# The second half's feed-forward products as pairs of 64-row products in the two halves of the array, each pair on two banks that are then crossed

## The chip, the cores and the metric

The kernel runs on one core of a Trainium2 chip. The metric is the device time of one execution in microseconds. Before the change, three runs gave a median of 1269.06 us (1267.8 to 1270.67).

## The reference: what is computed

A linear attention feeds a gated feed-forward layer. Eight batches of 576 tokens make 4608 tokens of 512 features (8 heads of 64); the hidden width is 1536.

```python
q_p, k_p = (phi(q), phi(k))                 # 64 -> 128, exp(+) and exp(-)
kv = np.einsum('bhsf,bhsd->bhfd', k_p, v)
num = np.einsum('bhsf,bhfd->bhsd', q_p, kv)
den = np.einsum('bhsf,bhf->bhs', q_p, z)[..., None] + 1e-06
x = (num / den)                              # as 4608 x 512
gate = 1.0 / (1.0 + np.exp(-(x @ w_gate)))
val = x @ w_val
out = (gate * val @ w_out).astype(np.float32)
```

## The kernel before

All large products are kept in float32r. Each operand is split in two, a high part and the rest (names ending in `h` and `l`), and each product is the sum of three: high by high, high by low, low by high.

The hidden width is cut into 12 blocks of 128, numbered j = 0 to 11. In the first half of the kernel, attention and blocks 0 to 3 run together; the feed-forward result of these four blocks is parked in DRAM (`yscr`). The second half, `rest_chunks` (L297 to L352), does blocks 4 to 11 for all tokens. It goes over 9 chunks C of 512 tokens, and in each over 8 blocks j: 72 steps. A step does, on TensorE:

- `mm_in` (L159) twice. The gate values g and the values v, each 128 hidden features by 512 tokens, each in a PSUM bank of its own, each the sum of 12 products: 4 slices of 128 input features, times the three of the split. The weight block is the stationary operand, the tokens x the moving one with 512 columns.
- `out_step` (L308) for the step before (`late`): for each of 4 groups of 128 tokens t, three products (`mm_out`, L169) of the gated values `hh`, `hl` (stationary) with the output weights (moving, 512 columns), added into bank `acc{t}`. The four banks `acc0` to `acc3` gather the 8 blocks of a chunk.

That makes 24 + 12 = 36 products of 512 columns a step, 2592 in all. After the v products of a step, `gated` (L177) turns g and v into `hh` and `hl`: Tanh and Exp of g on ScalarE (L182, L183), three operations on VectorE (L185 absolute value, L186 with v, L187), a cast to `hh` on ScalarE and the remainder `hl` on VectorE (`split`, L62 to L64). This chain runs while TensorE does the next products; its result is used only after the g and v products of the next step.

At the end of a chunk, four VectorE operations (L322) join the accumulators with the parked result, which SyncE fetched (L320), and the sums go to DRAM (L325). Also once a chunk, SyncE loads the tokens of a later chunk (L301), ScalarE casts them to `xh` and VectorE makes `xl` (`split`, 2048 columns each). The x tiles have two buffers, so this load starts when the chunk two before it has used its tokens for the last time.

The weights of blocks 4 to 11 come as float64 words. `load_weights` (L99) loads a tile of 512 KB (three buffers `wraw`), and `from_f64` (L76) rebuilds it with six VectorE operations (L81, L83, L88, L91, L94, L95) and one of ScalarE (L82); its high part goes through a DMA (L86) into `wh`. There are 24 such tiles, and those of the later blocks are rebuilt while the first chunk (C = 0) is running.

In the second half the order on TensorE is as written. The order on VectorE, ScalarE, SyncE and GpSimd is set by the scheduler at build time, from its own estimate of how long everything takes; each engine then runs its list in order.

Of the kernel before, what the change touches and what calls it, by code (L numbers as in the profile page):

```python
# [9 lines left out]
F32 = mybir.dt.float32  # L10
# [11 lines left out]
P = 128  # L22
# [23 lines left out]
def attention_moe(  # L46
# [19 lines left out]
    def behind(stack, marks):  # L66
        for m in marks:
            stack.enter_context(tc.issue_after(m.ins))
# [100 lines left out]
    def mm_out(acc, t, hs, j, first, last):  # L169
        (hh, hl, _), (wh, wl) = hs, weights[j]  # L170
        ts, ws = slice(t * P, t * P + P), slice(2 * DM, 3 * DM)
        for i, (a, w) in enumerate(((hh, wh), (hh, wl), (hl, wh))):
            nc.tensor.matmul(  # L173
                acc, a[:, ts], w[:, ws], start=first and i == 0, stop=last and i == 2
            )

    def gated(g, vl, w, mp, hb, name):  # L177
        u = mp.tile([P, w], F32, tag="u", name="u" + name)
        t = mp.tile([P, w], F32, tag="t", name="t" + name)
        hh = mp.tile([P, w], F32R, tag="hh", name="hh" + name, bufs=hb)  # L180
        hl = mp.tile([P, w], F32R, tag="hl", name="hl" + name, bufs=hb)
        act.activation(t, g, AF.Tanh, scale=0.5)  # L182
        act.activation(u, g, AF.Exp)  # L183
        tu = t.bitcast(U32)
        vec.tensor_scalar(tu, tu, 0x7FFFFFFF, None, op0=ALU.bitwise_and)  # L185
        vec.scalar_tensor_tensor(t, t, 1.0, vl, op0=ALU.add, op1=ALU.mult)  # L186
        vec.scalar_tensor_tensor(u, u, 1.0, t, op0=ALU.min, op1=ALU.mult)  # L187
        return hh, hl, split(hh, hl, u)
# [108 lines left out]
    def rest_chunks(js, xp, mp, ps_gv, ps_acc, load):  # L297
# [7 lines left out]
            split(xh, xl, raw)  # L305
            return xh, xl

        def out_step(C, i, hs):  # L308
            if i == 0:
# [4 lines left out]
            for t in range(CW // P):  # L314
                acc = accs[C][t]
                mm_out(acc, t, hs, js[i], i == 0, i == len(js) - 1)
                if i == len(js) - 1:
                    r = C * CW + t * P
                    y1 = mp.tile([P, DM], F32, tag="y1", name=f"yp_{C}_{t}", bufs=4)
                    nc.sync.dma_start(y1, yscr[r // CH][r % CH // P])  # L320
                    y = mp.tile([P, DM], F32, tag="y", name=f"y2_{C}_{t}", bufs=4)
                    vec.scalar_tensor_tensor(  # L322
                        y, acc, 0.5, y1, op0=ALU.mult, op1=ALU.add
                    )
                    nc.sync.dma_start(out[r : r + P, :], y)  # L325

        accs, late = {}, None
        for i, j in enumerate(js):
            if i == 1:
                with ExitStack() as stack:  # L330
                    behind(stack, marks)
                    xs = load_x(0)
            for m in range(3):
                marks = load(j, m)
        for C in range(NT // CW):
            nxt = None
            for i, j in enumerate(js):
                n = f"2_{C}_{j}"
                g = ps_gv.tile([P, CW], F32, tag="g", name="g" + n)
                vl = ps_gv.tile([P, CW], F32, tag="v", name="v" + n)  # L340
                mm_in(g, xs, j, 0, CW)
                mm_in(vl, xs, j, 1, CW)
                hs = gated(g, vl, CW, mp, 2, n)
                if late:
                    out_step(*late)
                late = (C, i, hs)
                if i == max(0, len(js) - 3) and (C + 1) * CW < NT:
                    with ExitStack() as stack:
                        behind(stack, () if C else marks)
                        nxt = load_x(C + 1)  # L350
            xs = nxt
        out_step(*late)  # L352


    ctx.enter_context(tc.manual_schedule(engines={mybir.EngineType.PE}))
    with ExitStack() as actx:
# [384 lines left out]
        def load(i):  # L741
            if i < N:
                load_k(i)
                load_q(i)
# [145 lines left out]
```

## Time and profile before

| | us |
|---|---|
| median of 3 runs | 1269.06 |
| the profiled execution, own time | 1269.45 |
| its span, first to last instruction | 1267.7 |
| TensorE matmul busy in the span | 1221.1 |
| VectorE busy | 788.4 |
| ScalarE busy | 522.6 |
| GpSimd busy | 0.7 |

1.75 us of the profiled execution lie outside its span. The second half begins at about 671 us and lasts to the end. PE is TensorE's matmul, PEld its weight loading, DVE VectorE, ACT ScalarE, POOL GpSimd, SP SyncE. Matmuls are pipelined: their recorded durations overlap, and the distance from start to start is the pace. A row of the timeline has the start, the time covered, the engine, the line, the operation, output and inputs, sizes, the count, and in brackets the idle time ahead of it and what ended it.

### The profile page before, as it was taken

The page shows a single profiled execution, that of the slowest core. Times are in us where ns is not written, and L with a number is a line of the kernel's source. Part 1 is how long each engine was busy: PE and PEld are TensorE (multiplying, and loading weights), DVE is VectorE, ACT ScalarE, POOL GpSimd, SP SyncE. Part 2 cuts the span into 40 slices and gives each one's busy share as a digit, 9 for nine tenths or more (in the row PEclk, how much of TensorE's full clock was granted, in tenths as well). Part 3 has the DMA queues.
Part 4 walks back from the last instruction along what each step waited for, and adds up shares of the span by engine and source line. Part 5 has one row for each costly group of instructions (what it writes and reads, how often), then busy time and mean ns, then how long its engine had stood idle before and what let it go on. Part 6 is the DMA issues. An engine that isn't in the chain of part 4 may idle for free.

```text
span 1267.7 us, 22794 instructions
## 1 busy us (share of the span) xinstructions
PE 1221.1 (96%) x9328; PEld 967.8 (76%) x9328; DVE 788.4 (62%) x1597; ACT 522.6 (41%) x1077; POOL 0.7 (0%) x6
## 2 busy tenths in 40 slices
PE   7778899999999999999989999999999999999998
PEld 4455577777778777777877888888888888888887
DVE  6998778887877878883997843424343434343333
ACT  4655555566656556564443322222222212222221
POOL 0000000000000000000000000000000000000000
PEclk9988899999999999999999999999999999999999
DMA  5567344343424334332756430203020202011010
GB/s 178 166 217 247 112 123 132 104 122 106 140 94 132 95 105 140 108 97 88 261 191 206 140 100 1 100 1 101 1 100 1 100 1 80 21 59 42 10 58 33
DMA packets 79123, 130.33 MB, mean 103 GB/s; under 512 B 17068, under 2 KB 36652, under 8 KB 79020
## 3 DMA queue, kind: packets, MB, share of 16 engines
q1 hardware_dynamic: 79020, 128.89, 31.5%
q8 instruction: 73, 1.20, 0.4%
q14 instruction: 30, 0.25, 0.1%
HBM read 90.86 MB, written 28.44 MB: 94 GB/s over the span
## 4 chain that ended last, share of the span: by engine, by line
PE 82%; DVE 12%; DMA 2%; ACT 2%; issue 1%; SPq 0%; DVEq 0%
PE acc L173 22%; PE g L166 16%; PE v L166 16%; PE gv L166 12%; PE kvz L537 5%; PE nm L589 4%; PE pq L420 2%; PE pk L430 2%; PE dp L602 2%; PE kvz L551 1%; PE pk L491 1%; DMA wraw<-w_moe 1%; DVE dk L454 1%; DVE mb L522 1%; DVE mx L441 1%
## 5 line engine op out<-in xcount | busy, mean ns | idle before, releaser
L173 PE MATMUL acc<-wh,hh 128*128 128x512 f32 x432 | 172.3, 399 | 3.2 <-ACT y L265 2.4
L166 PE MATMUL gv<-xh,wh 128*128 128x256 f32 x576 | 171.7, 298 | 0.0
L173 PE MATMUL acc<-wl,hh 128*128 128x512 f32 x432 | 169.2, 392 | 0.0
L166 PE MATMUL gv<-xl,wh 128*128 128x256 f32 x576 | 165.1, 287 | 4.0 <-DVE xl L213 4.0
L173 PE MATMUL acc<-wh,hl 128*128 128x512 f32 x432 | 168.7, 390 | 0.0
L166 PE MATMUL gv<-xh,wl 128*128 128x256 f32 x576 | 165.0, 287 | 0.0
L185 DVE TENSOR_SCALAR t<-t 128x512 uint32<-128x512 uint32 x72 | 30.7, 426 | 171.4 <-ACT t L182 171.1
L63 ACT CAST hh<-u 128x512 fp32r<-128x512 f32 x72 | 44.6, 619 | 219.8 <-DVE u L187 219.8
L166 PEld LDWEIGHTS gv<-xh,wh 128*128 128x128 f32 x576 | 112.0, 194 | 15.1 <-issue 13.1
L182 ACT ACTIVATE t<-g 128x512 f32<-128x512 f32 x72 | 43.0, 597 | 185.6 <-PE g L166 185.5
L166 PEld LDWEIGHTS gv<-xl,wh 128*128 128x128 f32 x576 | 112.2, 195 | 4.9 <-DVE xl L213 4.6
L166 PE MATMUL g<-xh,wh 128*128 128x512 f32 x288 | 113.0, 392 | 0.0
L166 PE MATMUL v<-xh,wh 128*128 128x512 f32 x288 | 112.6, 391 | 0.0
L166 PE MATMUL g<-xh,wl 128*128 128x512 f32 x288 | 112.5, 391 | 0.0
L166 PE MATMUL g<-xl,wh 128*128 128x512 f32 x288 | 112.5, 391 | 0.0
L166 PE MATMUL v<-xl,wh 128*128 128x512 f32 x288 | 112.3, 390 | 0.0
L166 PEld LDWEIGHTS gv<-xh,wl 128*128 128x128 f32 x576 | 112.2, 195 | 0.0
L166 PE MATMUL v<-xh,wl 128*128 128x512 f32 x288 | 112.1, 389 | 0.0
L186 DVE SCALAR_TENSOR_TENSOR t<-t,v 128x512 f32<-128x512 f32 x72 | 49.4, 686 | 97.9 <-PE v L166 97.9
L173 PEld LDWEIGHTS acc<-wh,hh 128*128 128x128 f32 x432 | 81.1, 188 | 26.6 <-issue 5.8
L173 PEld LDWEIGHTS acc<-wh,hl 128*128 128x128 f32 x432 | 81.1, 188 | 18.7 <-DVE hl L238 0.2
L173 PEld LDWEIGHTS acc<-wl,hh 128*128 128x128 f32 x432 | 81.3, 188 | 16.0
(99 smaller groups left out, 2136.8 us busy)
## 6 DMA issues: line engine op xcount, KB each, us to landing
wraw<-w_moe SPq DMA_DIRECT2D x36, 512.0 KB, 5.4
xl<-xs SPq DMA_DIRECT2D x34, 512.0 KB, 3.9
k<-k SPq DMA_DIRECT2D x32, 320.0 KB, 3.7
v<-v SPq DMA_DIRECT2D x32, 320.0 KB, 3.0
q<-q SPq DMA_DIRECT2D x32, 288.0 KB, 4.2
wh<-wtop SPq DMA_DIRECT2D x36, 256.0 KB, 2.3
ys<-y SPq DMA_DIRECT2D x36, 256.0 KB, 2.1
yp<-ys SPq DMA_DIRECT2D x36, 256.0 KB
```

The source lines that it names most:

```text
L63: a = act.copy(h, x)
L166: nc.tensor.matmul(o, a[:, ws], x[:, cs], start=i == 0, stop=i == 11)
L173: nc.tensor.matmul(acc, a[:, ts], w[:, ws], start=first and i == 0, stop=last and i == 2)
L182: act.activation(t, g, AF.Tanh, scale=0.5)
L185: vec.tensor_scalar(tu, tu, 0x7FFFFFFF, None, op0=ALU.bitwise_and)
L186: vec.scalar_tensor_tensor(t, t, 1.0, vl, op0=ALU.add, op1=ALU.mult)
L420: nc.tensor.matmul(pps[hd], wk[head(hd), :], x[head(hd), cs], start=True, stop=True)
L430: nc.tensor.matmul(pps[hd][:, t, :], kx[head(hd), t * P : t * P + P], wk[head(hd), :], start=True, stop=True,)
L441: vec.tensor_reduce(mx[:, :ns], pp[:, :ns, :], axis=AX.X, op=ALU.max, apply_absolute_value=True,)
L537: nc.tensor.matmul(kvz[o : o + Q, : 2 * F], vx[:, 2 * t + hd, o % D : o % D + Q], (e0, e1)[hd][:, t, :] if t < 4 else e2[:, 0, :], start=t ...
L589: nc.tensor.matmul(nms[hf][o : o + Q, :], w[:, sg, o : o + Q], es[sg][:, o // D, cs], start=sg == 0, stop=sg == 1, tile_position=(0, o),)
L602: nc.tensor.matmul(dp[o : o + Q, :], w[:, 2, z : z + Q], es[sg][:, hd, hf * HS : hf * HS + HS], start=sg == 0, stop=sg == 1, tile_position ...
```

## The change

Every product of 128 contracted rows in the second half becomes two of 64 rows: one in the upper half of the array (rows 0 to 63), one in the lower (rows 64 to 127). The new `halves_mm` issues them in pairs, an upper and a lower one in turn, and the two of a pair fill different banks. In one pass g takes its upper rows while v takes its lower rows; in a later pass the banks are crossed, v above and g below. The out products do the same with `acc0`, `acc1` against `acc2`, `acc3`. A step is now: 12 pairs for g above and v below, 6 pairs of the first half of `out_half` for the step before, 12 pairs for v above and g below, 6 pairs of its second half. `gated` comes after all four, so g and v end together, and its result is used after the 12 pairs of the next step's first pass. Only the very first step has no step before it and keeps its whole products.

Where a bank changes from one half of the array to the other, the new code puts a memset of one element on GpSimd (`marks`) that waits for the last product of the old half, and the first product of the new half waits for the memset. This makes 10 such memsets in nearly every step.

```diff
+    ROWS = slice(0, P // 2), slice(P // 2, P)
...
+    def halves_mm(top, bottom):
+
+        for pair in zip(top, bottom):
+            for r, (o, (a, x), start, stop) in enumerate(pair):
+                rs = ROWS[r]
+                mm = nc.tensor.matmul(o, a[rs, :], x[rs, :], start=start, stop=stop).ins
+                before = None if start else fills.get(id(o))
+                if before and before[1] != r:
+                    mark = marks.tile([1, 1], F32, tag="mark", name="mark")
+                    turn = pool.memset(mark, 0.0).ins
+                    for later, sooner in ((turn, before[0]), (mm, turn)):
+                        tc.add_manual_dep(
...
+                fills[id(o)] = mm, r, o
...
+        def out_half(C, i, hs, n):
...
+            parts = [
+                [
+                    x
+                    for t in ts
+                    for x in group(accs[C][t], terms_out(t, hs, js[i]), first, last)
+                ]
+                for ts in ((0, 1), (2, 3))
+            ]
+            halves_mm(*(parts[::-1] if n else parts))
...
-                mm_in(g, xs, j, 0, CW)
-                mm_in(vl, xs, j, 1, CW)
-                hs = gated(g, vl, CW, mp, 2, n)
                 if late:
-                    out_step(*late)
-                late = (C, i, hs)
+                    tg, tv = (terms_in(xs, j, m, CW) for m in range(2))
+                    halves_mm(group(g, tg, start=True), group(vl, tv, start=True))
+                    out_half(*late, 0)
+                    halves_mm(group(vl, tv, stop=True), group(g, tg, stop=True))
+                    out_half(*late, 1)
+                else:
+                    mm_in(g, xs, j, 0, CW)
+                    mm_in(vl, xs, j, 1, CW)
+                late = (C, i, gated(g, vl, CW, mp, 2, n))
...
-        out_step(*late)
+        for n in range(2):
+            out_half(*late, n)
```

TensorE, chunk 4, block 7, before: the last g product, the first and last lines of the v products, and what follows. (In the names `g2_4_7` is the g bank of chunk 4, block 7; `acc2_4_0` the accumulator of its first 128 tokens; the last number is only a count.)

```order
L166 MATMUL v2_4_7_10845<-xh2_4_10569,wh7_8842 128x512
L166 MATMUL v2_4_7_10845<-xl2_4_10570,wh7_8842 128x512
L166 MATMUL v2_4_7_10845<-xh2_4_10569,wl7_8843 128x512
L173 MATMUL acc2_4_0_10779<-wh6_8807,hh2_4_6_10823 128x512
L173 MATMUL acc2_4_0_10779<-wl6_8808,hh2_4_6_10823 128x512
L173 MATMUL acc2_4_0_10779<-wh6_8807,hl2_4_6_10824 128x512
L173 MATMUL acc2_4_1_10780<-wh6_8807,hh2_4_6_10823 128x512
```

TensorE at the same place with the change: the end of the first half of `out_half`, and then the first pairs of the crossed pass.

```order
L200 MATMUL acc2_4_1_12532<-wl6_8811,hh2_4_6_12702 128x512
L200 MATMUL acc2_4_3_12534<-wl6_8811,hh2_4_6_12702 128x512
L200 MATMUL acc2_4_1_12532<-wh6_8810,hl2_4_6_12703 128x512
L200 MATMUL acc2_4_3_12534<-wh6_8810,hl2_4_6_12703 128x512
L200 MATMUL v2_4_7_12712<-xh2_4_12164,wh7_8845 128x512
L200 MATMUL g2_4_7_12711<-xh2_4_12164,wh7_8845 128x512
L200 MATMUL v2_4_7_12712<-xl2_4_12165,wh7_8845 128x512
L200 MATMUL g2_4_7_12711<-xl2_4_12165,wh7_8845 128x512
```

Upper and lower products alternate, and each has a bank of its own. The v products now end only after the out products' first half, and next to the g products.

VectorE where chunk 0 passes into chunk 1, before. `xl2_2` is the token tile of chunk 2, `t2_1_4`, `u2_1_4`, `hl2_1_4` the gate chain of the first step of chunk 1, and `y2_0_0` to `y2_0_3` the four joins of chunk 0.

```order
L64 TENSOR_TENSOR xl2_2_9726<-xl2_2_9726,xh2_2_9725 128x2048
L185 TENSOR_SCALAR t2_1_4_9434<-t2_1_4_9434 128x512
L322 SCALAR_TENSOR_TENSOR y2_0_0_9449<-acc2_0_0_9091,yp_0_0_9447 128x512
L186 SCALAR_TENSOR_TENSOR t2_1_4_9434<-t2_1_4_9434,v2_1_4_9408 128x512
L322 SCALAR_TENSOR_TENSOR y2_0_1_9457<-acc2_0_1_9092,yp_0_1_9455 128x512
L322 SCALAR_TENSOR_TENSOR y2_0_2_9465<-acc2_0_2_9093,yp_0_2_9463 128x512
L187 SCALAR_TENSOR_TENSOR u2_1_4_9433<-u2_1_4_9433,t2_1_4_9434 128x512
L322 SCALAR_TENSOR_TENSOR y2_0_3_9473<-acc2_0_3_9094,yp_0_3_9471 128x512
L64 TENSOR_TENSOR hl2_1_4_9436<-u2_1_4_9433,hh2_1_4_9435 128x512
```

The same place with the change.

```order
L64 TENSOR_TENSOR xl2_2_10441<-xl2_2_10441,xh2_2_10440 128x2048
L228 TENSOR_SCALAR t2_1_4_9909<-t2_1_4_9909 128x512
L229 SCALAR_TENSOR_TENSOR t2_1_4_9909<-t2_1_4_9909,v2_1_4_9795 128x512
L372 SCALAR_TENSOR_TENSOR y2_0_0_9890<-acc2_0_0_9083,yp_0_0_9888 128x512
L230 SCALAR_TENSOR_TENSOR u2_1_4_9908<-u2_1_4_9908,t2_1_4_9909 128x512
L372 SCALAR_TENSOR_TENSOR y2_0_1_9895<-acc2_0_1_9084,yp_0_1_9893 128x512
L372 SCALAR_TENSOR_TENSOR y2_0_2_9900<-acc2_0_2_9085,yp_0_2_9898 128x512
L372 SCALAR_TENSOR_TENSOR y2_0_3_9905<-acc2_0_3_9086,yp_0_3_9903 128x512
L64 TENSOR_TENSOR hl2_1_4_9911<-u2_1_4_9908,hh2_1_4_9910 128x512
```

The same operations stand there; the first join has moved behind the second operation of the gate chain, and the third operation of the chain ahead of the second join. The remainder `hl2_1_4` stands last in both.

VectorE in the first chunk, before: the remainder of the first step and what follows. `wtop` and `wraw` are the weight tiles being rebuilt.

```order
L64 TENSOR_TENSOR hl2_0_4_9046<-u2_0_4_9043,hh2_0_4_9045 128x512
L81 TENSOR_SCALAR wtop9_0_8916<-wraw9_0_8914 128x512
L88 TENSOR_SCALAR wraw8_2_8901<-wraw8_2_8901 128x512
L185 TENSOR_SCALAR t2_0_5_9081<-t2_0_5_9081 128x512
L91 SCALAR_TENSOR_TENSOR wraw8_2_8901<-wraw8_2_8901 128x512
L83 SCALAR_TENSOR_TENSOR wtop9_0_8916<-wraw9_0_8914,wtop9_0_8916 128x512
L94 TENSOR_SCALAR wraw8_2_8901<-wtop8_2_8903 128x512
```

VectorE with the change, ahead of the same operation `t2_0_5`. Between `hl2_0_4` and `t2_0_5` now stand 24 rows of weights, of which these are the last seven; before there are two.

```order
L95 SCALAR_TENSOR_TENSOR wl9_8916<-wraw9_1_8928 128x512
L88 TENSOR_SCALAR wraw9_2_8939<-wraw9_2_8939 128x512
L81 TENSOR_SCALAR wtop10_0_8954<-wraw10_0_8952 128x512
L91 SCALAR_TENSOR_TENSOR wraw9_2_8939<-wraw9_2_8939 128x512
L94 TENSOR_SCALAR wraw9_2_8939<-wtop9_2_8941 128x512
L83 SCALAR_TENSOR_TENSOR wtop10_0_8954<-wraw10_0_8952,wtop10_0_8954 128x512
L95 SCALAR_TENSOR_TENSOR wl9_8916<-wraw9_2_8939 128x512
L228 TENSOR_SCALAR t2_0_5_9148<-t2_0_5_9148 128x512
L88 TENSOR_SCALAR wraw10_0_8952<-wraw10_0_8952 128x512
L81 TENSOR_SCALAR wtop10_1_8965<-wraw10_1_8963 128x512
L229 SCALAR_TENSOR_TENSOR t2_0_5_9148<-t2_0_5_9148,v2_0_5_9058 128x512
```

The scheduler now puts the weights of blocks 8 to 10 ahead of the second step's gate chain. From `hl2_0_5` to `hl2_0_6` it puts 27 rows of weights between (before: 12), and all weights are done by `hl2_0_6` but for one row; before, they are spread over the steps to block 9.

More of the change, by code (lines that the diff above doesn't have):

```diff
@@ L175, in mm_out, with terms_in, terms_out, group @@
             )
+    ROWS = slice(0, P // 2), slice(P // 2, P)
+    def terms_in(xs, j, m, w):
+        (xh, xl), (wh, wl) = xs, weights[j]
+        return [
+            (a[:, m * DM + cc * P : m * DM + cc * P + P], x[:, cc * w : cc * w + w])
+            for cc in range(NC4)
+            for a, x in ((wh, xh), (wh, xl), (wl, xh))
+        ]
+    def terms_out(t, hs, j):
+        (hh, hl, _), (wh, wl) = hs, weights[j]
+        ts, ws = slice(t * P, t * P + P), slice(2 * DM, 3 * DM)
+        return [(a[:, ts], w[:, ws]) for a, w in ((hh, wh), (hh, wl), (hl, wh))]
+    fills = {}
+    marks = ctx.enter_context(tc.tile_pool(name="marks", bufs=4))
+    def halves_mm(top, bottom):
[9 more added lines that the diff above has]
+                        tc.add_manual_dep(
+                            later,
+                            sooner.name,
+                            mybir.DependencyInfo(
+                                mybir.DependencyClass.Sync, mybir.DependencyReason.DATA
+                            ),
+                            reason="other rows of the array fill the same bank",
+                        )
+                fills[id(o)] = mm, r, o
+    def group(o, terms, start=False, stop=False):
+        n = len(terms) - 1
+        return [(o, ax, start and i == 0, stop and i == n) for i, ax in enumerate(terms)]
     def gated(g, vl, w, mp, hb, name):
@@ L306, in load_x @@
             return xh, xl
[L308 to L309 removed]
+        def out_half(C, i, hs, n):
+            if n == 0 and i == 0:
                 accs[C] = [
@@ L313, in out_step @@
                 ]
[L314 to L325, printed above, removed]
+            first, last = n == 0 and i == 0, n == 1 and i == len(js) - 1
+            parts = [
[5 more added lines that the diff above has]
+                for ts in ((0, 1), (2, 3))
+            ]
+            halves_mm(*(parts[::-1] if n else parts))
+            for t in range(CW // P if last else 0):
+                r = C * CW + t * P
+                y1 = mp.tile([P, DM], F32, tag="y1", name=f"yp_{C}_{t}", bufs=4)
+                nc.sync.dma_start(y1, yscr[r // CH][r % CH // P])
+                y = mp.tile([P, DM], F32, tag="y", name=f"y2_{C}_{t}", bufs=4)
+                vec.scalar_tensor_tensor(
+                    y, accs[C][t], 0.5, y1, op0=ALU.mult, op1=ALU.add
+                )
+                nc.sync.dma_start(out[r : r + P, :], y)
         accs, late = {}, None
@@ L330, in rest_chunks @@
                 with ExitStack() as stack:
-                    behind(stack, marks)
+                    behind(stack, loaded)
                     xs = load_x(0)
             for m in range(3):
-                marks = load(j, m)
+                loaded = load(j, m)
         for C in range(NT // CW):
```

2 lines of the change are left out of this document (1 added, 1 removed).

## The prediction

> **What bounds the kernel now.** I read the page's shares first, then the stretches of the second half, then who waits there, then the timeline for the pace.
>
> ```profile
> PE 1221.1 (96%) x9328; PEld 967.8 (76%) x9328; DVE 788.4 (62%) x1597; ACT 522.6 (41%) x1077; POOL 0.7 (0%) x6
> ...
> PE 82%; DVE 12%; DMA 2%; ACT 2%; issue 1%; SPq 0%; DVEq 0%
> ```
>
> TensorE is busy for 96% of the span and carries 82% of the chain that ended last. Two stretches of the second half (busy us of PE, PEld, DVE, ACT, POOL; clock; DMA share; GB/s), and then all that TensorE waited for from 671 us to the end, by the list of waits:
>
> ```profile
> 679.40:718.90 39.50, 39.50 (x175) 32.52 (x174) 38.56 (x80) 15.86 (x25) 0.00 (x0) 1.00 0.60 198
> 800.00:900.00 100.00, 100.00 (x439) 82.23 (x438) 39.25 (x59) 23.99 (x38) 0.00 (x0) 1.00 0.18 60
> ...
> PEld acc L173 <- DVE hl L64: 0.2, 1, 0.2
> ```
>
> The second half is TensorE alone: it waits 0.2 us in all, at full clock. VectorE has plenty of room from 800 us on (39%), but none in the first chunk (38.56 of 39.5 us), where it rebuilds weights. The pace comes from the timeline: products of 512 columns inside a step, and products of 256 columns from the first half.
>
> ```profile
> 404.05 0.28 PE L166 MATMUL gv<-xh,wh 128*128 128x256 f32 x1
> 404.17 0.28 PE L166 MATMUL gv<-xl,wh 128*128 128x256 f32 x1
> 404.29 0.28 PE L166 MATMUL gv<-xh,wl 128*128 128x256 f32 x1
> ...
> 900.02 0.39 PE L166 MATMUL g<-xh,wl 128*128 128x512 f32 x1
> ...
> 901.39 0.39 PE L166 MATMUL g<-xh,wl 128*128 128x512 f32 x1
> ...
> 902.99 0.39 PE L166 MATMUL v<-xh,wh 128*128 128x512 f32 x1
> ```
>
> From 900.02 to 902.99 are 13 products: 0.2285 us each, 8.23 us for a step of 36. At 256 columns it is 0.120. So 256 columns cost 0.1085 us, and a product has a fixed part of 0.2285 - 0.217 = 0.0115 us. That bubble is the only thing in the pace that another arrangement of the same columns could win.
>
> **The change part by part.**
>
> *The pairs.* 2592 - 24 products become 2568 pairs, each streaming the 512 columns of one old product. Nothing in this trace runs float32r in half-array pairs; the nearest rows are the first half's float32 products of 64 rows, alternating between the halves and between banks:
>
> ```profile
> 405.05 0.50 PE L430 MATMUL pk<-wk,k 64*128 64x128 f32 x6
> 405.27 0.39 PE L430 MATMUL pk<-wk,k 64*128 64x128 f32 x4
> 405.49 0.66 PE L420 MATMUL pq<-q,wk 64*128 64x288 f32 x4
> ...
> L420 PE MATMUL pq<-q,wk x256: 402/403/844, 6.2 to 555.6; 64*128 64x288 f32 x128
> ```
>
> Two pairs of `pk` start every 0.22 us, 0.11 a pair. For `pq`, four products cover 0.66 us and the last lasts 0.403, so the second pair starts 0.25 us after the first. A whole product's pace is its recorded duration less 0.16 (0.39 against 0.2285, 0.28 against 0.120); by that a single `pq` would take 0.24. So two halves do run side by side, loads included, for the price of one, plus 0 to 0.009 us. From `pk` to `pq` 160 columns cost 0.14 us, 0.00088 a column, so `pk`'s 128 columns take 0.112: no bubble is left there. But these columns take twice as long as float32r's, and a bubble could hide under them. Bounds for a float32r pair: 0.217 us (bubble hidden) to 0.2285 + 0.009. I take 0.2285, the row of the same type and columns: each half has its own bubble, at the same time as the other's. Term: 0; ends -0.0115 x 2568 = -29.5 us and +23 us.
>
> The Trainium skill (TensorE: Matmul & The Clock Gate, Part 3, "Measured speedup vs the span model") has a pack last as long as one product plus about 4 ns for each further tile; by that the term is an estimated +10 us and the sum 1323, since slower pairs give 2 us of the waits below back. The `pq` row allows it, and does not show it for this type.
>
> *The gate chain in an ordinary step.* Before, g ends 12 products ahead of v and the result is used 36 products after v. Now both end together, and the result is needed after 6 + 12 pairs. Rows of one free chain:
>
> ```profile
> 901.82 0.60 ACT L182 ACTIVATE t<-g 128x512 f32<-128x512 f32 x1 [3.36 <-PE g L166]
> 902.45 0.43 DVE L185 TENSOR_SCALAR t<-t 128x512 uint32<-128x512 uint32 x1 [3.26 <-ACT t L182]
> ...
> 929.33 0.69 DVE L186 SCALAR_TENSOR_TENSOR t<-t,v 128x512 f32<-128x512 f32 x1 [1.69 <-PE v L166]
> 930.12 0.69 DVE L187 SCALAR_TENSOR_TENSOR u<-u,t 128x512 f32<-128x512 f32 x1
> 930.84 0.62 ACT L63 CAST hh<-u 128x512 fp32r<-128x512 f32 x1 [3.18 <-DVE u L187]
> 931.50 0.69 DVE L64 TENSOR_TENSOR hl<-u,hh 128x512 fp32r<-128x512 f32 x1 [0.69 <-ACT hh L63]
> ```
>
> Let s be the start of the last product. Tanh starts at s + 0.43 (901.39 to 901.82), L185 at s + 1.06, L186 0.53 later (its 0.43 and 0.10 between dependent operations, as from 929.33 to 930.12), then 2.17 from L186 to the start of `hl`, and 0.69: s + 4.45. With 0.14 for the hand-off and the weight load, 4.6. `hl` is first used by the third pair of the out half, at s + 21 x 0.2285 = 4.80. It fits, by 0.2 us. Term: 0.
>
> *The chunk boundary, 8 times.* VectorE's rows there, before:
>
> ```profile
> 935.25 1.91 ACT L63 CAST xh<-xl 128x2048 fp32r<-128x2048 f32 x1 [3.78 <-DMA xl<-xs]
> ...
> 937.19 2.29 DVE L64 TENSOR_TENSOR xl<-xl,xh 128x2048 fp32r<-128x2048 f32 x1 [5.00 <-ACT xh L63]
> 939.40 0.42 DVE L185 TENSOR_SCALAR t<-t 128x512 uint32<-128x512 uint32 x1
> 939.73 0.68 DVE L322 SCALAR_TENSOR_TENSOR y<-acc,yp 128x512 f32<-128x512 f32 x1
> 940.34 0.68 DVE L186 SCALAR_TENSOR_TENSOR t<-t,v 128x512 f32<-128x512 f32 x1
> ...
> 943.50 0.69 DVE L64 TENSOR_TENSOR hl<-u,hh 128x512 fp32r<-128x512 f32 x1
> ```
>
> The x load waits for the old chunk's last use of its buffer, at 929.33 - 0.43 = 928.90, and `xl` ends at 939.48: 10.58 us later, ahead of the gate chain on VectorE. One step of 8.23 us later the new chunk's first g and v end, so L185 can start at s + 2.27 instead of s + 1.06 (it overlaps `xl` by 0.08). Then, in the new order, L186 0.53 later and six rows (`y`, L187, three `y`, `hl`) at 0.60 apart (939.73 to 940.34): `hl` ends 4.82 after L185, at s + 7.09, usable at 7.23. TensorE wants it at 4.80: 2.43 us late. Before, the use came 36 products and two more after v, which covered all this. Seven boundaries: 17; the last has no x load, so L185 starts at 1.06 and `hl` is usable at 6.02: 1.2. Term: +18 us.
>
> *The first chunk.* Rows after the first step's chain, and the load of a weight tile:
>
> ```profile
> 676.79 0.39 PE L166 MATMUL g<-xh,wh 128*128 128x512 f32 x1
> ...
> 680.08 0.43 DVE L81 TENSOR_SCALAR wtop<-wraw 128x512 uint32<-128x512 uint32 x1
> 680.42 0.42 DVE L88 TENSOR_SCALAR wraw<-wraw 128x512 uint32<-128x512 uint32 x1
> ...
> 681.09 0.69 DVE L91 SCALAR_TENSOR_TENSOR wraw<-wraw 128x512 uint32<-128x512 uint32 x1
> 681.70 0.69 DVE L83 SCALAR_TENSOR_TENSOR wtop<-wraw,wtop 128x512 uint32<-128x512 uint32 x1
> ...
> wraw<-w_moe SPq DMA_DIRECT2D x36, 512.0 KB, 5.4
> ```
>
> A short row takes 0.335 us, a long one 0.60. In the new order 33 rows stand between `hl2_0_4` and `hl2_0_5`: 17 short and 16 long, 15.3 us; from 680.08, `hl2_0_5` starts at 695.4 and is usable at 696.2. TensorE's second step begins at 676.79 as before, and the third pair of the third step's first out half is due 36 + 12 + 2 pairs later, at 688.2: 8 us late at least. The tiles must also be loaded: 5.4 us into one of three buffers that VectorE holds about 5 us, 3.5 us a tile against 2.8 of work (three short rows, three long). Two loads come late, by about 2 us each: 12. From `hl2_0_5` to `hl2_0_6` are 30 rows, 14 short and 16 long, 14.3 and `hl` itself 0.6, against a step of 8.23: 6.7 late, with the loads up to 11. Then no weights are left. Both ends: 14.7 to 23; I take 23, since the loads' 5.4 us are a row. Before, the same rows were spread so that TensorE never waited; nothing gives the time back.
>
> *The clock.* TensorE now stops for about ten microseconds, twice. The nearest stop:
>
> ```profile
> 131.58 1.32 PE L420 MATMUL pq<-q,wk 64*128 64x288 f32 x2 [4.42 <-ACT d L482]
> ...
> 131.10:137.90 6.80, 6.32 (x36) 4.42 (x40) 5.05 (x10) 3.91 (x11) 0.00 (x0) 0.50 0.57 174
> ```
>
> After 4.42 us of idling the clock is 0.50 for 6.8 us, which costs up to 3.4 us. The first stop's loss vanishes in the second. Term: +2.5 (0 to 5).
>
> *The end.* The last chain is needed after 6 pairs, at s + 7 x 0.2285 = 1.6; `hh` is usable at 3.9. Before, 12 products covered it but for the 0.2 us quoted. Term: +2.
>
> *The memsets.* 10 a step on an idle GpSimd, 0.12 us each by its 0.7 us for 6. The shortest cover is at the crossing of g and v, 7 pairs (1.6 us) from the last product of the old half to the first of the new, less its 0.39: 1.2 us for two hand-offs and a memset. VectorE and ScalarE take 0.03 us for one (902.42 to 902.45). No row shows GpSimd's; term 0, upper end 0.3 us at 71 crossings, 21.
>
> Sum: 0 + 18 + 23 + 2.5 + 2 = 45.5. The profiled execution took 1269.45 us, 0.4 over the median of the runs: 1315.
>
> **The rivals.**
>
> *Faster: the bubble hides.* Place: every pair. Price -29.5 us. For: `pk` leaves no bubble. Against: the waits must then stay under 29.5, and their lower ends are 14.7 + 18 + 2 = 35; at this pace they grow. It decides only if both long stops shrink to half: about 1260. 4%; no change, 1%.
>
> *The bubble hides, the waits stay.* At 0.217 a boundary is 3.1 us late, in all 23; first chunk 24, end 2, clock 2.5, ordinary steps 1: 1269.5 - 29.5 + 52.5 = 1292. 24%. The Trainium skill (TensorEngine Tiling (Array Packing), Performance Considerations, "When to Use Tiling") keeps row tiling for contractions of at most 64; here 128 rows are contracted and the array is full already. By that rule there is nothing to win, and this rival falls; the `pq` pair's 0.25 against 0.24 agrees, for another type.
>
> *A pair costs 0.009 us more than a product.* +23; waits 41: 1333. 10%.
>
> *GpSimd's memsets come late.* +21: 1336. 5%.
>
> *The halves take turns at the rate of float32r.* The `pk` columns at half rate do not exclude it. 0.457 a pair: +587, and the waits vanish under it: 1858. The new VectorE list, with 24 rows of weights in one step, looks made for such steps; that is the scheduler's estimate. 8%.
>
> **How the numbers follow.** The forecast itself has 48%: 1315, with 1304 to 1325 from its own ends (14.7 instead of 23 in the first chunk, the clock 0 to 5, the boundaries by 1 us each). The range runs from below the hidden bubble to above the late memsets, 1285 to 1342, and leaves out the serial case, the faster one and the tails. Slower by over 0.2% (2.5 us, about what a measurement of this kernel tells from no change): all but 6%.
>
> **What would show it.** Right: 0.2285 us from pair to pair with the upper and lower starts a few ns apart; two gaps of about 10 us on TensorE near 688 and 706, ended by `hh` or `hl` of blocks 5 and 6; at seven boundaries 2 to 3 us ended by `hh` and `hl` with `y` rows ahead of them; clock 0.5 after the long gaps. Wrong: pairs at 0.217 or at 0.457; gaps ended by `mark`; no gap in the first chunk.

## The result and the profile after

The changed kernel takes 1324.83 us (median of 3 runs, 1324.02 to 1325.35) against 1269.06 before: a ratio of 1.0438, with a 95% interval of 1.0414 to 1.0461. It is slower by 55.8 us. The profiled execution took 1325.35 us, its span is 1323.6.

The page of the changed kernel: the shares, the chain of work that ended last, and the load of a weight tile.

```profile
PE 1250.6 (94%) x11896; PEld 991.3 (75%) x11896; DVE 790.1 (60%) x1597; ACT 524.9 (40%) x1077; POOL 55.9 (4%) x688
...
PE 74%; DVE 14%; DMA 5%; issue 3%; ACT 3%; SPq 0%; DVEq 0%; POOL 0%; ACTq 0%; POOLq 0%
...
wraw<-w_moe SPq DMA_DIRECT2D x36, 512.0 KB, 4.7
```

TensorE's share of the chain that ended last fell from 82% to 74%, and VectorE, DMA and "issue" took what it lost. What it waited for in the second half, by the list of waits (total us, times, longest):

```profile
PE acc L200 <- issue: 15.8, 2, 8.3
PE acc L200 <- ACT hh L63: 6.8, 7, 2.1
PE acc L200 <- DVE hl L64: 3.7, 8, 0.5
```

Before, the same list held 0.2 us. All three rows are the first products of an out half, which need `hh` and `hl`. The two long waits stand under "issue", and the timeline of the first of them shows what was late: the gate chain of the second step of chunk 0, between rows of weights on VectorE.

```profile
688.12 0.43 DVE L81 TENSOR_SCALAR wtop<-wraw 128x512 uint32<-128x512 uint32 x1 [0.62 <-DMA wraw<-w_moe]
...
689.03 0.39 PE L200 MATMUL v<-xh,wl 64*128 64x512 f32 x1
...
693.67 0.42 DVE L228 TENSOR_SCALAR t<-t 128x512 uint32<-128x512 uint32 x1
...
695.03 0.68 DVE L229 SCALAR_TENSOR_TENSOR t<-t,v 128x512 f32<-128x512 f32 x1
...
696.96 0.62 ACT L63 CAST hh<-u 128x512 fp32r<-128x512 f32 x1 [1.08 <-DVE u L230]
...
697.68 0.79 PE L200 MATMUL acc<-wh,hh 64*128 64x512 f32 x2 [8.26 <-issue]
```

TensorE starts its last pair at 689.03, and the next product 0.10 us after the cast to `hh` ends (696.96 + 0.62). From start to start that is 8.65 us; the second stop, at 716.3, is 7.88. The chunk boundary with the longest stop of the eight, from the tokens' remainder `xl` to the new chunk's first `hl`:

```profile
1179.79 2.29 DVE L64 TENSOR_TENSOR xl<-xl,xh 128x2048 fp32r<-128x2048 f32 x1 [4.72 <-ACT xh L63]
...
1182.00 0.42 DVE L228 TENSOR_SCALAR t<-t 128x512 uint32<-128x512 uint32 x1
...
1182.96 0.39 PE L200 MATMUL v<-xh,wl 64*128 64x512 f32 x1
1183.13 0.68 DVE L372 SCALAR_TENSOR_TENSOR y<-acc,yp 128x512 f32<-128x512 f32 x1
...
1184.33 1.88 DVE L372 SCALAR_TENSOR_TENSOR y<-acc,yp 128x512 f32<-128x512 f32 x3
1184.45 0.62 ACT L63 CAST hh<-u 128x512 fp32r<-128x512 f32 x1 [3.71 <-DVE u L230]
...
1185.12 1.05 PE L200 MATMUL acc<-wh,hh 64*128 64x512 f32 x2 [1.77 <-ACT hh L63]
...
1185.66 0.18 PEld L200 LDWEIGHTS acc<-wh,hh 64*128 64x128 f32 x1 [0.37 <-DVE y L372]
...
1186.13 0.68 DVE L64 TENSOR_TENSOR hl<-u,hh 128x512 fp32r<-128x512 f32 x1
1186.86 0.50 PE L200 MATMUL acc<-wh,hl 64*128 64x512 f32 x2 [0.46 <-DVE hl L64]
```

The gate chain starts as `xl` ends, four joins `y` push in between, and TensorE stops first for `hh` (1.77 us), then for the banks of `acc` that the joins still read (0.37 us at the weight load), then for `hl` (0.46). The clock behind such stops (columns as in the stretches of the prediction):

```profile
692.70:702.90 10.20, 5.22 (x24) 3.74 (x26) 9.34 (x19) 2.57 (x5) 0.25 (x4) 0.50 0.62 208
713.20:720.00 6.80, 3.69 (x18) 3.11 (x20) 5.20 (x7) 2.42 (x2) 0.25 (x4) 0.50 0.12 44
1187.60:1191.00 3.40, 3.40 (x18) 2.62 (x18) 0.00 (x0) 0.00 (x0) 0.14 (x3) 0.50 0.93 326
```

Last, the pairs, an ordinary step of the changed kernel:

```profile
899.93 0.39 PE L200 MATMUL v<-xh,wh 64*128 64x512 f32 x1
899.95 0.39 PE L200 MATMUL g<-xh,wh 64*128 64x512 f32 x1
900.16 0.39 PE L200 MATMUL v<-xl,wh 64*128 64x512 f32 x1
900.18 0.39 PE L200 MATMUL g<-xl,wh 64*128 64x512 f32 x1
...
902.45 0.39 PE L200 MATMUL v<-xh,wl 64*128 64x512 f32 x1
902.46 0.39 PE L200 MATMUL g<-xh,wl 64*128 64x512 f32 x1
```

The two halves run side by side, 10 to 20 ns apart, and a pair follows the last after 0.229 us here. The mean over all 2,497 distances from pair to pair at full clock is 231.3 ns; for the 2,591 distances of before it is 228.6.

So the 55.9 us between the two spans are, from the starts of all products in both traces:

| | us | forecast |
|---|---|---|
| pairs slower by 2.7 ns, 2,591 times | 7.0 | 0 |
| two stops in the first chunk | 16.1 | 23 |
| eight boundaries | 17.1 | 18 |
| half clock behind stops | 10.8 | 2.5 |
| the end: last chain 2.3, behind the last product 1.4 | 3.7 | 2 |
| the second half starts later | 1.2 | 0 |
| sum | 55.9 | 45.5 |

### The profile page after: what moved, and what is told of

Its sections match the earlier page's. It is cut to its first block, busy times and chain, and to the rows that moved or that the text cites. A ratio compares the mean times of both kernels' runs of the same rounds, so it can differ in the third digit from the quotient of the medians.

```text
span 1323.6 us, 29024 instructions
## 1 busy us (share of the span) xinstructions
PE 1250.6 (94%) x11896; PEld 991.3 (75%) x11896; DVE 790.1 (60%) x1597; ACT 524.9 (40%) x1077; POOL 55.9 (4%) x688
## 4 chain that ended last, share of the span: by engine, by line
PE 74%; DVE 14%; DMA 5%; issue 3%; ACT 3%; SPq 0%; DVEq 0%; POOL 0%; ACTq 0%; POOLq 0%
PE v L200 14%; PE acc L200 14%; PE g L200 13%; PE gv L166 11%; PE acc L173 6%; PE kvz L592 4%; PE nm L644 4%; PE pq L475 2%; DMA xl<-xs 2%; PE pk L485 2%; PE dp L657 2%; DVE y L372 1%; PE kvz L606 1%; DVE xl L64 1%; DVE mb L577 1%
## 5 line engine op out<-in xcount | busy, mean ns | idle before, releaser
L200 PE MATMUL g<-xh,wh 64*128 64x512 f32 x568 | 223.9, 394 | 0.0
L200 PE MATMUL v<-xh,wh 64*128 64x512 f32 x568 | 223.9, 394 | 0.0
L200 PE MATMUL g<-xl,wh 64*128 64x512 f32 x568 | 223.8, 394 | 0.0
L200 PE MATMUL v<-xl,wh 64*128 64x512 f32 x568 | 223.8, 394 | 0.0
L200 PE MATMUL g<-xh,wl 64*128 64x512 f32 x568 | 223.0, 393 | 0.0
L200 PE MATMUL v<-xh,wl 64*128 64x512 f32 x568 | 223.0, 393 | 0.0
L200 PE MATMUL acc<-wh,hh 64*128 64x512 f32 x576 | 122.1, 401 | 23.0 <-issue 15.8
L200 PE MATMUL acc<-wh,hl 64*128 64x512 f32 x576 | 118.4, 402 | 3.7 <-DVE hl L64 3.7
L200 PE MATMUL acc<-wl,hh 64*128 64x512 f32 x576 | 119.7, 399 | 0.0
L200 PEld LDWEIGHTS v<-xh,wh 64*128 64x128 f32 x568 | 106.4, 187 | 11.6
L200 PEld LDWEIGHTS g<-xh,wl 64*128 64x128 f32 x568 | 105.9, 186 | 10.8
```

The lines of the kernel that those rows point to most:

```text
L200: mm = nc.tensor.matmul(o, a[rs, :], x[rs, :], start=start, stop=stop).ins
```

## Experiments

Three theories stood against each other. The theory of the prediction: the time is waits for the gate's result, because the new order asks for it earlier and VectorE's list delivers it later; pairs themselves cost nothing and win nothing. Rival A: the pairs are dearer in themselves, by the pair, the crossing or its memsets. Rival B: the order does no harm, the loss is in the first chunk alone. (In the first four expectations "rival B" means the memsets, which belong to rival A here.) Times are medians of 3 rounds (4 to 6 runs) beside the kernel before on the same chip (1269.2 to 1270.2 us); ratios are to that.

**The new order with whole products** (`order_whole`). Each bank gets six whole products in each pass; no halves, no crossings, no memsets.

```diff
-halves_mm(group(g, tg, start=True), group(vl, tv, start=True))
+whole_mm(group(g, tg[:6], start=True), group(vl, tv[:6], start=True))
...
-halves_mm(group(vl, tv, stop=True), group(g, tg, stop=True))
+whole_mm(group(vl, tv[6:], stop=True), group(g, tg[6:], stop=True))
```

> No half-array products and no memsets: whole 128-row products in the new order of a step (half of g and v in turn, the out products of two token groups, the other half of g and v, the out products of the other two, and only then the gate chain). Theory: most of the loss is in the order: pace 0.2285 us, boundaries about as late as in the change (10 to 18 us in all, with half clock behind them about 5), a first chunk with 21, 18 and 20 rows between the remainders instead of 33 and 30 (4 to 8 us), the end 2.5: about 1293 us. Rivals A and B: 1269 to 1275 us.

Measured: 1295.39 us, ratio 1.0197 (1.018 to 1.0214); 1293 was expected. What TensorE waited for:

```profile
PE acc L173 <- ACT hh L63: 12.8, 13, 2.0
PE acc L173 <- DVE hl L64: 1.6, 3, 0.6
```

With no pair in it, the order alone costs some 25 us, and the same two releasers show. That contradicts rival A as the whole story. A product takes 229.2 ns here.

**Chunk 0 whole, in the old order** (`c0whole`). The pairs begin with chunk 1.

```diff
-                if late:
+                if C:
...
+                    hs = gated(g, vl, CW, mp, 2, n)
+                    if late:
+                        out_whole(*late)
+                    late = (C, i, hs)
```

> Chunk 0 alone keeps the whole products in the old order (gate chain ahead of the out products), chunks 1 to 8 are as in the change. VectorE's list in the first chunk is then that of the kernel before. Theory: the two stops in the first chunk (8.4 and 7.7 us in the changed kernel's trace) and the half clock behind them (about 4.5 us) go, the boundaries stay: 1304 us. Rival A (the pairs themselves): one step in nine is whole again, a ninth of the loss goes, about 1319 us. Rival B (memsets): likewise about 1319 us.

Measured: 1298.2 us, ratio 1.0218 (1.0202 to 1.0233); 1304 was expected.

```profile
PE acc L200 <- ACT hh L63: 5.5, 7, 2.1
PE acc L200 <- DVE hl L64: 3.7, 8, 0.5
```

The two stops are gone and the boundaries have stayed. Of the 26.6 us that went, the two stops and their half clock were 20.5 in the changed kernel's trace (16.1 and 4.4). Most of the rest isn't the first chunk's: behind the boundaries and the end there are two stretches of half clock instead of four (3.1 us), and the second half starts 2.3 us earlier in this trace. Rival B falls, since some 28 us are left over the kernel before.

**The result used a step later** (`lag2`). `hh` and `hl` get a third buffer, and the first two steps stay whole.

```diff
-                    out_half(*late, 0)
+                    old = late.pop(0)
+                    out_half(*old, 0)
...
-                late = (C, i, gated(g, vl, CW, mp, 2, n))
+                late.append((C, i, gated(g, vl, CW, mp, 3, n)))
```

> All pairs, crossings and memsets as in the change, but the out products take the result of the step two before (three buffers for hh and hl instead of two), so that a gate chain has 36 pairs more until it is used; the first two steps keep whole products. Theory (the change is slow because TensorE waits for gate chains that the new order needs 18 pairs after g and v, while the pairs themselves cost only about 3 ns each): the waits at the eight chunk boundaries go (2.4 us late against 8.3 us more cover), and with them the half clock behind them; of the two stops in the first chunk 2 to 5 us are left, since VectorE's list still has 28 and 26 rows in two steps; about 1282 us. Rival A (the half-array pairs themselves cost the time, whatever they wait for): about 1320 us. Rival B (the memsets on GpSimd hold the crossings): no change against the changed kernel, about 1325 us.

Measured: 1297.43 us, ratio 1.0215 (1.02 to 1.023): a miss by 15 us.

```profile
PE g L200 <- ACT u L226: 8.0, 1, 8.0
PE v L200 <- DVE t L229: 2.5, 2, 1.7
PE acc L200 <- DVE y L372: 1.7, 8, 0.2
```

The waits for `hh` and `hl` are gone at every boundary, as the theory has it. But in chunk 0 a stop has come back in another place: g has two banks, and the first g product of the sixth step waits 8.0 us for the Exp (`u`) of the fourth, which still reads its bank. ScalarE's list, from the last weight rows to that Exp:

```profile
711.88 0.72 ACT L82 ACTIVATE wtop<-wtop,ebias 128x512 uint32<-128x512 uint32 x1 [2.21 <-DVE wtop L81]
714.88 1.90 ACT L63 CAST xh<-xl 128x2048 fp32r<-128x2048 f32 x1 [2.28 <-DMA xl<-xs]
...
717.17 0.59 ACT L226 ACTIVATE u<-g 128x512 f32<-128x512 f32 x1
```

The Exp stands behind weight rows that wait for VectorE and behind the cast of the next tokens, which waits for their load. More lag hides the length of a chain, but not a list of other work that stands ahead of the chain's start for longer than the banks last.

**Both together** (`lag2_c0whole`: the two edits above in one kernel).

```diff
-                if late:
+                if C:
+                    old = late.pop(0)
...
+                    late.append((C, i, gated(g, vl, CW, mp, 3, n)))
+                    if len(late) == 3:
+                        out_whole(*late.pop(0))
```

> Each result of the gate is used two steps behind its products instead of one, and chunk 0 stays in the old order with whole products, so both kinds of wait that the new order makes are taken away together. The theory (the time goes to waits for hh and hl at the chunk boundaries and behind the first weights, each with a slow clock behind it, and a small part to the pairs' pace): the stops near 690 to 720 us and the waits for hh and hl at the boundaries go, the eight waits of some 0.6 us for the banks of acc stay, and the pairs stay at 231 ns, 2.3 ns over whole products: 8 x 0.6 + some 2,200 x 0.0023 = 10 us over the kernel before: 1279 us, 1275 to 1284. Rival A (pairs cost more in themselves than a whole product, by 10 ns or more): 1290 or more. Rival B (the order is no cause, the loss is in the first chunk alone): 1298, as the kernel with chunk 0 whole was.

Measured: 1282.12 us, ratio 1.0102 (1.0081 to 1.0124), inside the expectation and under rival A's bound. Taking both kinds of wait away gives back 43 of the 55.8 us.

**No later token loads** (`no_xload`). From chunk 2 on the tokens of chunk 0 or 1 are used again, so those outputs are computed from other tokens.

```diff
-                        nxt = load_x(C + 1)
+                        nxt = load_x(C + 1) if C == 0 else both[(C + 1) % 2]
```

> The changed kernel, but from chunk 2 on the second half takes the tokens of chunk 0 or 1 again: it leaves out the later loads of tokens with their rounding and remainders, so those chunks of the output are computed from other tokens. The question is what delays hh and hl at a chunk boundary: the pieces of work for the next chunk's tokens on ScalarE and VectorE, or the four final scalings of acc on VectorE and the gate's own chain. If the tokens' pieces are half of it: boundaries 15 us to some 7, and the half clock behind three of them (some 1.6 us each) goes: 1312 us. If the tokens' pieces are all of it: 1304. If they are none of it (they have been done long before the boundary): 1324, no change.

Measured: 1311.92 us, ratio 1.0336 (1.0314 to 1.0359); 1312 was expected.

```profile
PE acc L200 <- issue: 15.7, 2, 8.1
PE acc L200 <- DVE hl L64: 3.7, 8, 0.5
PE acc L200 <- ACT hh L63: 2.1, 1, 2.1
```

The six boundary waits for `hh` are gone (the one left is the end's), the eight of 0.46 us for `hl` behind the joins have stayed, and no boundary is followed by half clock any more. So the new tokens' work makes `hh` late. The run takes out the cast on ScalarE along with `xl` on VectorE; that it is `xl` is read from the boundary shown above, where the gate chain starts as `xl` ends and ScalarE idles for 3.71 us ahead of `hh`. That the joins make `hl` late is read from the same rows; no run takes the joins away.

**Pairs without crossing** (`nocross`). Each bank keeps its half in both passes, so half the terms are taken twice and half left out; no memsets are needed.

```diff
-            halves_mm(*(parts[::-1] if n else parts))
+            halves_mm(*parts)
...
-                    halves_mm(group(vl, tv, stop=True), group(g, tg, stop=True))
+                    halves_mm(group(g, tg, stop=True), group(vl, tv, stop=True))
```

> As the change, but the second pass and the second out half aren't crossed: g and acc0, acc1 stay in the upper half of the array and v and acc2, acc3 in the lower, so the upper or lower rows are taken twice and the other rows of each product are left out; there are no memsets on GpSimd and no waits for them. Theory: the memsets lie under 7 or more pairs, so nothing changes: 1324 us, within 4 us (VectorE's list in the first chunk has 30 and 32 rows instead of 33 and 30). Rival B (the memsets hold the crossings): faster by 10 us or more, and the pairs come at 0.2285 us.

Measured: 1314.37 us, ratio 1.0346 (1.0328 to 1.0363), 10 us under the changed kernel: the expectation missed, and rival A had a point. A stretch without a stop, the changed kernel (its matmuls in brackets):

```profile
775.00:835.00 60.00, 60.00 (x522) 1.00 0.06 19
```

and the same stretch without crossing:

```profile
775.00:835.00 60.00, 60.00 (x526) 1.00 0.09 28
```

Four more matmuls fit in, near one in a hundred. Over all distances a pair takes 229.1 ns against 231.3, with no wait to see: 5.7 us over 2,592 pairs. About 4 us more is less half clock. The next four runs look for the 2.2 ns.

**Uncrossed pairs with the memsets back** (`nocross_marks`). The terms are those of the last kernel; each memset waits for the other half's last product, as in the changed kernel.

```diff
+                other = pair[1 - r][0]
+                before = None if start or id(o) in seen else prior.get(id(other))
+                seen.add(id(o))
```

> The uncrossed pairs of the earlier run (upper rows for one bank and lower rows for the other in both passes, so half the terms are taken twice and half left out), but with the memsets on GpSimd put back in the same places and numbers as in the changed kernel: each waits for the other half's last product and the next product of this half waits for it. It tells apart the two causes of the 2.2 ns by which a pair took longer in the changed kernel (231.3 against 229.1 ns uncrossed). If it is the hand-off (memset and the two waits): 231 ns, and 1320 to 1325 us. If it is the crossing of the banks itself: 229.1 ns and 1314 us.

Measured: 1319.52 us, ratio 1.0391 (1.0355 to 1.0428), and 231.3 ns. It is not the crossing.

**Only g and v crossed** (`cross_gv`). Two hand-offs a step are left of ten; for the banks of `acc` half the terms are taken twice.

```diff
-            halves_mm(*(parts[::-1] if n else parts))
+            halves_mm(*parts)
```

> The changed kernel with only the banks of g and vl crossed; the four banks of acc keep their half in both passes (there too the one half's terms are taken twice and the other's left out), and their eight hand-offs a step go, two of ten are left. If the 2.2 ns belong to each hand-off: mean 229.5 ns a pair, 1316 us. If they belong to every pair on a crossed bank: 231 ns for the pairs of g and vl, 229 for those of acc, mean 230.5, 1320 us. If they have another cause: no change from either kernel.

Measured: 1318.7 us, ratio 1.0391 (1.0362 to 1.042), and again 231.3 ns, for the uncrossed pairs of `acc` as for the others. The first two expectations both fail: the cost is there in full with a fifth of the hand-offs. In the kernels with chunk 0 whole, the whole products of that chunk, far from any memset, were slower too. What all these kernels share, and the ones at 229 ns lack, is the four tiles of one element that the memsets write: they are allocated early, and tiles that are allocated behind them lie elsewhere in SBUF.

**The kernel before with these tiles, and no use of them** (`before_place`), and **with two hand-offs a step** (`before_marks`). Whole products, old order.

```diff
+    turns = ctx.enter_context(tc.tile_pool(name="turns", bufs=4))
+    def mark(sooner=None):
+        t = turns.tile([1, 1], F32, tag="mark", name="mark")
+        turn = pool.memset(t, 0.0).ins
...
+    for _ in range(4):
+        mark()
```

```diff
-                mm_in(g, xs, j, 0, CW)
-                mm_in(vl, xs, j, 1, CW)
+                two = [mm_in(g, xs, j, 0, CW), mm_in(vl, xs, j, 1, CW)]
...
-                    out_step(*late)
+                    out_step(*late, [mark(mm) for mm in two])
```

> The kernel before with whole products and the old order, and only the four tiles of the memsets added where the changed kernel has them, with four memsets at the very start and none later. Two kernels with 2 and with 10 hand-offs a step both took 231.3 ns a pair, one with none took 229.1, and in the kernels whose chunk 0 was whole the whole products were slower too (230.1 to 231.5 ns against 227.8 to 229.3 before): so the 2.2 ns do not go by the hand-off's count. Theory P (place): the tiles move everything allocated behind them in SBUF, and products read their data a little slower from there: 231 ns, 2,592 x 0.0022 = 5.7 us: 1275 us. Theory H (hand-off: what GpSimd or TensorE do while memsets run): 228.6 ns, 1269 us.

> The kernel before with whole products and the old order, and two memsets a step on GpSimd: each waits for the last product of g or vl, and the first product of acc 2 or 3 waits for it, some 2 us later, so that nothing stops. The four tiles are there as in the kernel sent with it. Theory H (the hand-offs slow the products near them or all of them): 231 ns, 1275 us, while the kernel with the tiles alone stays at 1269. Theory P (place): both take 1275. Neither: both 1269, and then the 2.2 ns need pairs and memsets together.

Measured: 1274.39 us, ratio 1.0032 (1.002 to 1.0044), for the tiles alone; 1275.03, ratio 1.005 (1.0022 to 1.0078), with hand-offs. The second half of the kernel before, and of the one with the idle tiles:

```profile
725.00:1265.00 540.00, 538.99 (x2358) 1.00 0.14 46
```

```profile
725.00:1265.00 540.00, 540.00 (x2342) 1.00 0.14 45
```

The same products at the same full clock, 16 fewer in the stretch, although the stream of before ends 1 us ahead of the stretch's end. From start to start they take 230.7 ns in the mean instead of 228.6, and 230.7 with the hand-offs too. So the tiles alone cost the 2.1 ns; the hand-offs cost nothing more.

The 2.1 ns are a mean over products that changed very differently. The same step (chunk 3, block 8) in the kernel before and with the idle tiles:

```profile
899.79 0.39 PE L166 MATMUL g<-xl,wh 128*128 128x512 f32 x1
...
903.22 0.39 PE L166 MATMUL v<-xl,wh 128*128 128x512 f32 x1
```

```profile
899.83 0.40 PE L166 MATMUL g<-xh,wl 128*128 128x512 f32 x1
...
903.10 0.40 PE L166 MATMUL v<-xl,wh 128*128 128x512 f32 x1
```

Before, the 15 products between these starts take 0.2287 us each; with the tiles, the 14 take 0.2336. Sorted by the block whose weights they use, from the starts of all products at full clock:

| mean ns from start to start | before | `before_place` | changed kernel | `lag2_c0_noplace` |
|---|---|---|---|---|
| g and v, blocks 4 to 7 | 227.5 | 227.5 | 228.8 | 228.6 |
| g and v, blocks 8 to 11 | 229.2 | 233.3 | 233.3 | 229.3 |
| out products, blocks 4 to 7 | 228.9 | 233.3 | 233.2 | 229.2 |
| out products, blocks 8 to 11 | 229.2 | 229.3 | 230.4 | 229.8 |

The last column is the next run. In `before_place` the means of a block repeat to 0.2 ns in chunks 1 to 8, and blocks 6 to 11 have them in chunk 0 as well, where VectorE rebuilds weights; so what the other engines do at the time does not decide. In the programs as built, the four tiles take 128 bytes of each partition. They move `hh`, `hl` and the weights of blocks 8 to 11 by that; the weights of blocks 4 to 7 and the tokens stay. So the two slow rows are the products whose stationary operand has moved by 128 bytes against the moving one.

**Both waits gone, and the tiles gone** (`lag2_c0_noplace`). The memsets write a tile that exists anyway; crossings and hand-offs stay.

```diff
-    marks = ctx.enter_context(tc.tile_pool(name="marks", bufs=4))
...
-                    mark = marks.tile([1, 1], F32, tag="mark", name="mark")
-                    turn = pool.memset(mark, 0.0).ins
+                    turn = pool.memset(ebias[0:1, :], -896.0 * 2.0**23).ins
```

> The kernel with results used two steps later and chunk 0 whole (1282.1 us, 231.1 ns a pair), with the memsets written into a tile that exists anyway, so that the four small tiles are gone and everything behind them lies in SBUF where it lay before; crossings, hand-offs and order stay. Theory P (the 2.2 ns belong to the place of the tiles): 229.0 ns a pair, 2,593 x 0.0021 = 5.4 us less: 1276.7 us, 1275 to 1279, ratio 1.006 to the kernel before; what is left are the eight waits of 0.6 us at the boundaries and the end. Theory H (hand-offs or crossings cost it in pairs after all): 1282, 231 ns.

Measured: 1277.38 us, ratio 1.0061 (1.0045 to 1.0078); 1276.7 was expected. Matmuls in 510 us, first with the four tiles, then without:

```profile
760.00:1270.00 510.00, 508.52 (x4382) 1.00 0.13 42
```

```profile
760.00:1270.00 510.00, 508.38 (x4417) 1.00 0.13 42
```

The pairs are back at 229.2 ns. The expectation is not quite right about the place: the third buffers of `hh` and `hl` still move the weights of blocks 8 to 11, by 4096 bytes in the program as built; the pace shows no cost of it. With the waits of the first chunk and those for `hh` and `hl` gone, and the tiles too, the pairs, crossings and memsets are still 7.5 us slower than whole products. Of this 1.5 us lie behind the last product, and most of the rest is 0.8 us a chunk (66.50 us from the joins of one chunk to those of the next, 65.67 before); about half of that is the wait for the joins, 0.6 us where a pair has 0.23. None of the kernels beats the one before.

**The pairs in the old order** (`old_order`): both passes of g and v, then both passes of `acc`.

```diff
-                    out_half(*late, 0)
                     halves_mm(group(vl, tv, stop=True), group(g, tg, stop=True))
-                    out_half(*late, 1)
...
+                hs = gated(g, vl, CW, mp, 2, n)
+                if late:
+                    out_half(*late, 0)
+                    out_half(*late, 1)
```

> The changed kernel's pairs, crossings and memsets, but in the order of before: both passes of g and vl, then both passes of acc, so that a bank is crossed right behind its last product. It prices what the new order was taken for. By the theory the waits for hh and hl at the boundaries go (the result is wanted 24 pairs behind its products again), the first chunk's stops shrink to some 11 us with 3 of slow clock, the pace is 231 ns (6 us), and the crossing of g and vl now stands open: some 0.5 us a step (0.3 to 1.0), 71 steps: 35 us (21 to 70). Sum 1269 + 6 + 14 + 35 = 1324, 1305 to 1360. If the hand-off is hidden even there, 1289; then the new order cost 25 us for nothing.

Measured: 1341.24 us, ratio 1.0561 (1.0544 to 1.0579): inside the range, 17 above its middle. The hand-off now stands open, once a step:

```profile
PE v L200 <- POOL mark L204: 18.9, 71, 0.4
```

One of them on the timeline: the last product of v below, the memsets, the first products of v above.

```profile
899.06 0.39 PE L200 MATMUL v<-xh,wl 64*128 64x512 f32 x1
899.57 0.27 POOL L204 MEMSET mark<- 1x1 f32 x6 [4.08 <-PE v L200]
899.71 0.50 PE L200 MATMUL v<-xh,wh 64*128 64x512 f32 x1 [0.27 <-POOL mark L204]
900.05 0.40 PE L200 MATMUL v<-xl,wh 64*128 64x512 f32 x1
```

From the last product below to the first above are 0.65 us, where a pair has 0.23, and the next start comes 0.1 late as well; a tenth more is lost at the banks of `acc`. That is near 0.65 us a step, 71 times: 46. So the new order is not for nothing. It hides the hand-off, and costs waits for the gate in its place; the sum is 16 us in its favour.

## Why the prediction was right, and where its terms were off

The sign, the place and the releasers were as forecast: the pairs win nothing, and the new order makes TensorE wait for the gate. 1315 was forecast, 1324.8 came, inside the range. By its steps:

- *The pairs.* Taking 0.2285 us, each half with a bubble of its own at the same time as the other's, was right: uncrossed pairs take 229.1 ns and whole products in the same order 229.2. By the Trainium skill (TensorE: Matmul & The Clock Gate, Part 3, "Measured speedup vs the span model") it would have been an estimated 4 ns more. These two means show no such cost here. The hidden bubble, the halves that take turns and the dearer pair fall as rivals. What the step lacked was no property of pairs: +2.1 ns a product in the mean from four tiles that move others in SBUF, 5.4 of the 7.0 us; the rest, 0.5 ns, whole products in the new order have as well. The forecast looked for the memsets' price at their waits, and the price was in their tiles.
- *The ordinary step.* Right: between the boundaries the list of waits holds nothing.
- *The chunk boundary.* 18 forecast, 17.1 measured, with the releasers as worked out. The split was different: at six of the eight TensorE stopped for `hh`, with 0.6 to 2.2 us from start to start, and the banks of `acc` were a stop of their own, which the step did not name.
- *The first chunk.* The stops came where they were expected, 16.1 us instead of 23. The step that failed is the loads: 12 and 11 counted two tiles late by 2 us each. In this trace a tile lands in 4.7 us instead of 5.4, and the longest wait of VectorE for one near the two stops is 0.62 us. Without the loads its lower end, 14.7, was nearly it.
- *The clock.* The worst sized term: 2.5 forecast, 10.8 measured. It looked for half clock behind the two long stops alone. Those gave 4.4; three boundaries gave 1.6 each, though none of their single gaps is longer than 2.2 us, and the end 1.6.
- *The end.* 2.3 for the last chain, as forecast; 1.4 more behind the last product were not in it. The four joins start 0.26 us ahead of it (1317.85 of 1318.11); before, they started 1.62 ahead (1261.98 of 1263.60), since the banks of `acc` were finished one after the other.
- *The memsets.* The hand-off's cover held: no wait ends with `mark` in the changed kernel. Uncovered it costs 0.45 us, as `old_order` shows.

The misses have both signs (-6.9 in the first chunk; +8.3 clock, +7.0 pace, +1.7 end, +1.2 start, -0.9 boundaries), which is why the sum is nearer than its parts. That much of the closeness is luck.

## What to carry to other kernels

Splitting a full contraction over the two halves of the array leaves the column count as it is, and each half has its own fixed part: there was nothing to win here, only an order to pay for. When an order asks for a result earlier, price the lists of the engines that make it at their fullest places (chunk boundaries, the first chunk), not in the ordinary step, and allow for half clock behind stops of 1 to 2 us as well (three of eight boundaries here). Before a small difference spread over all products is put down to the change's idea, run the old kernel with only the new tiles allocated, and compare the pace by the tiles that the products read.

## What was not expected of the hardware

- **Place in SBUF.** Four one-element tiles, never used, slow the 512-column products of the second half by 2.1 ns (0.9%) in the mean, at full clock and with no wait to see. It isn't all of them: g and v of blocks 8 to 11 and the out products of blocks 4 to 7 go to 233.3 ns, the others keep their mean (table at `before_place`). The ten traces of kernels with the tiles all have 232.9 to 233.3 ns in these two groups, the four without them 228.9 to 229.6, whole products and pairs alike. The first half's 256-column products did not change (near 119.7 ns in both). A shift by 4096 bytes showed no cost (229.3 ns, `lag2_c0_noplace`). Which other steps in address count was not tried. That it is the distance between the two operands, and not something else that an added tile changes, fits all these rows and is still an inference.
- **The clock's stretches.** From the first long stop to the last product, the half-clock stretches of the changed kernel are 10.24, 6.83, and four times 3.41 us long, all multiples of 3.41. The Trainium skill (TensorE: Matmul & The Clock Gate, Part 1, "What's actually happening") has the clock follow windows of about 3.4 us that run freely; the lengths agree. Boundaries with gaps of 1.25, 1.17 and 2.17 us were followed by half clock, one of 1.24 was not, so the length of a gap alone does not decide it here.
- **The two of a pair are not tied to one start.** The second product of a pair starts between 0 and 45 ns after the first, drifting from pair to pair; pairs that start under 10 ns apart come every 231.4 ns, those 20 to 29 ns apart every 231.3.
